# Windowed attention and a GELU MLP on one core: the first MLP product of six of nine tiles by seven block products, and queries and keys handled by pairs of heads

## The chip, the core and the metric

The kernel runs on one core of a Trainium2 chip. The metric is the device time of one execution in microseconds, as the median of several runs; lower is better. A core has five engines with one instruction queue each, worked off in order: TensorE (PE: matmuls, and their weight loads, PEld), VectorE (DVE), ScalarE (ACT), GpSimd (POOL) and SyncE (SP, which only issues DMAs here). They wait for one another through semaphores. Matmul results land in PSUM, which has eight banks of 128 x 512 float32; everything else lies in SBUF or in DRAM.

## What is computed

Eight batches of attention, 8 heads, 576 positions, 64 values per head. Each position sees itself and the 127 before it, with a linear bias per head. The 4608 rows of 512 values that come out go through an MLP of width 2048 with an exact GELU. The core of the reference:

```python
scores = scale * np.matmul(q, k.transpose(0, 1, 3, 2))
mask = (rel >= 0) & (rel < window)                       # window = 128
scores = np.where(mask, scores + bias[None], -1000000000.0)
attn = softmax(scores)
x = np.matmul(attn, v).transpose(0, 2, 1, 3).reshape(B * S, H * D)     # 4608 x 512
h = x @ w_in                                             # 512 x 2048
g = 0.5 * h * (1.0 + erf(h * inv_sqrt2))
return (g @ w_out).astype(np.float32)                    # 2048 x 512
```

## The kernel before

**Two float16 numbers for one float32.** TensorE multiplies float16 at full rate. So nearly every operand is split: it is scaled by a power of two, `hi` is it rounded to float16, `lo` is what is left, rounded to float16 (`low_part`, L144, a DVE operation; `hi` is made by ACT or POOL). A product a*b is then three float16 products, hi*hi + lo*hi + hi*lo, added up in one PSUM bank. The scale comes from the largest absolute value of a whole operand: `absmax` (L212) over each partition, `over_partitions` (L106 to L126) over the 128 partitions, `pow2` (L128) and `inverse` (L138). `over_partitions` of most operands is a chain of small DVE operations: four copies, a reduction, a 32 x 32 transpose, a reduction, a copy, a transpose, and four maxima. Batch 0 of the attention and the second product of tile 0 work in float32.

**The tiles.** The 4608 rows are nine tiles of 512 tokens (`TT`). Tile t needs the attention of batches t - 1 and t, since 576 is more than 512. For each tile there are two stages on TensorE:

- the h stage, `mlp_in` (L577): 16 blocks `fc` of 128 of the 2048 columns. A block takes 12 matmuls (L584) of 128 x 512: four chunks `cc` of the 512 inputs, three products each, into one of the four PSUM banks with the tag `mm`. ACT takes the GELU out of the bank (L600) into a buffer of the tag `ob` (three of them), POOL makes its `hi` (L601), DVE its `lo` (L602, which runs at L145).
- the o stage, `mlp_out` (L612): four blocks `tb` of 128 tokens with 48 matmuls (L622) each, whose results ACT or DVE scale (L630, L632) and SP sends out (L633).

Both stages have 192 matmuls of 128 x 512.

**The attention beside them.** While tile t runs, the attention of batch b = t + 1 is computed. It has four units, one for each pair of heads. A unit is: `scores` (L370), 54 matmuls on quarters of the array (L399) into banks with the tag `att`, five DVE operations that scale them, add the bias and put them into a tile `s` of SBUF (L421); `softmax` (L484), two DVE reductions for the maxima (L491), nine exponentials on ACT (L494), the divisions, `hi` on POOL (L500) and `lo` on DVE (L502), and two transposing DMAs (L503) into `et`; and `weigh` (L515), 54 or more matmuls (L540) whose results go to the tiles `x` of t = b and b + 1 as `hi` by ACT (L553) and `lo` by DVE (L554). The tag `s` has two buffers. ACT has to load another table of functions (ACT_TABLE_LOAD) when it goes from GELU to exponentials or back.

Queries and keys of a batch are loaded whole (L339 to L343: two DMAs into the two buffers of the tag `ld`), and `split_qk` (L345) takes their maxima and splits them into `qbuf` and `kbuf`, 128 x 2304 each, which the units of the batch read.

**What sets the order.** The main loop (L731 to L768) emits the work step by step: step 0 to 15 are `mlp_in`, 16 to 31 quarters of `mlp_out`. `SCORES_AT` and `WEIGH_AT` say at which steps the scores and the weighing of the units are emitted. A scheduler then places the instructions of all engines; by `high_priority` some are moved ahead. What it leaves is a fixed queue for each engine.

## Time and profile before

| | |
|---|---|
| median of 3 runs | 957.98 us (956.48 to 960.62) |
| the profiled execution: its time | 957.65 us |
| its span, first to last instruction | 955.8 us |
| granted TensorE clock, mean | 0.988 |
| DMA moved | 91.18 MB, in 172451 packets |

All times below are of this one execution, counted from the start of its span. The tiles stand in it one behind the other; a tile's h stage begins with its first matmul of L584:

| tile | h stage from | o stage from | until |
|---|---|---|---|
| 0, and all before it | 66.46 | 111.50 | 187.92 |
| 1 | 187.92 | 236.86 | 294.16 |
| 2 | 294.16 | 345.53 | 395.85 |
| 3 | 395.85 | 443.66 | 493.71 |
| 4 | 493.71 | 542.11 | 592.29 |
| 5 | 592.29 | 639.18 | 689.23 |
| 6 | 689.23 | 736.02 | 786.13 |
| 7 | 786.13 | 827.57 | 869.01 |
| 8 | 869.01 | 910.45 | 955.80 |

Tiles 7 and 8 have no attention beside them. How to read the views: the table of windows gives, for each stretch, the busy time of each engine with its number of instructions; a row of the groups gives an instruction's line, engine, operation, operands with shapes, how often, then its busy time and mean duration in ns, and then the idle time of its engine just before it, with what ended it. A matmul's duration includes the time until its result has landed, so matmuls overlap one another, and their pace is the distance of their starts.

### The profile page before, as it was taken

Reading aid. Unit: us, or ns where it says so; the run is one execution under the profiler, and the core shown is the slowest. Engines: PE = TensorE matmul, PEld = TensorE weight load, DVE = VectorE, ACT = ScalarE, POOL = GpSimd, SP = SyncE. Lnnn points to the kernel's source line nnn. Section 1 sums busy time; section 2 is a strip of 40 time slices with the busy share of each in tenths; the row PEclk is TensorE's granted clock in tenths of the full one; section 3 lists DMA queues with packets and bytes.
Section 4 is the critical chain, followed back from the end, with each engine's and each line's share of the span. In section 5 each row is a group of like instructions: output and inputs, shape, how many; then the busy total and the mean of one; then the engine's idle time right before and its main releaser. Section 6 shows DMA issues by size and latency. Waiting matters only on the chain.

```text
span 955.8 us, 17566 instructions
## 1 busy us (share of the span) xinstructions
PE 920.2 (96%) x7036; PEld 450.0 (47%) x7036; DVE 634.8 (66%) x1254; ACT 449.5 (47%) x957; POOL 253.5 (27%) x516
## 2 busy tenths in 40 slices
...
GB/s 324 199 96 244 222 50 74 132 188 100 72 135 166 76 51 106 193 32 66 79 193 45 66 95 171 56 79 95 73 28 51 86 81 1 1 23 23 0 12 34
DMA packets 172451, 91.18 MB, mean 95 GB/s; under 512 B 132561, under 2 KB 153169, under 8 KB 172241
## 3 DMA queue, kind: packets, MB, share of 16 engines
...
## 4 chain that ended last, share of the span: by engine, by line
PE 68%; DVE 8%; ACT 4%; DMA 3%; issue 2%; POOL 1%; SPq 0%; POOLq 0%; ACTq 0%; DVEq 0%
PE o L622 31%; PE h L584 29%; PE av L540 4%; PE sc L399 3%; DMA et<-e_main 2%; ACT s L494 2%; DVE e_main L145 2%; DVE s L421 1%; DVE g L145 1%; DVE nmax L491 1%; DVE stq L213 1%; POOL e_main L500 1%; DMA q<-qp 1%; DVE wo L145 1%; DMA v<-vp 1%
## 5 line engine op out<-in xcount | busy, mean ns | idle before, releaser
L584 PE MATMUL h<-x,wi 128*128 128x512 f16 x1728 | 381.8, 379 | 5.0 <-ACT g L600 3.3
L584 PEld LDWEIGHTS <-wi 128*128 128x128 f16 x1728 | 166.2, 98 | 205.8 <-issue 7.3
L622 PE MATMUL o<-wo,g 128*128 128x512 f16 x1152 | 260.2, 380 | 0.0
L622 PEld LDWEIGHTS <-g 128*128 128x128 f16 x1536 | 145.9, 98 | 175.2 <-issue 0.7
L601 POOL TENSOR_SCALAR g<-g,sg 128x512 f16<-128x512 f32 x128 | 104.2, 818 | 286.1 <-ACT g L600 280.4
L494 ACT ACTIVATE s<-s,nmax 128x192 f32<-128x192 f32 x252 | 111.2, 442 | 121.4 <-DVE nmax L491 114.4
L145 DVE SCALAR_TENSOR_TENSOR g<-g,sg,g 128x512 f16<-128x512 f32 x128 | 106.1, 841 | 90.4 <-POOL g L601 90.3
L500 POOL TENSOR_SCALAR e_main<-s,z 128x192 f16<-128x192 f32 x252 | 121.4, 499 | 126.1 <-issue 43.6
L600 ACT ACTIVATE g<-h,gs 128x512 f32<-128x512 f32 x128 | 86.0, 686 | 135.0 <-PE h L584 108.6
L145 DVE SCALAR_TENSOR_TENSOR e_main<-s,z,e_main 128x192 f16<-128x192 f32 x252 | 111.0, 482 | 15.3 <-POOL e_main L500 14.8
L622 PE MATMUL o<-wo_first,g 128*128 128x512 f16 x384 | 88.3, 379 | 0.0
L399 PE MATMUL sc<-kbuf,qbuf 64*64 64x192 f16 (+1 forms) x1656 | 73.3, 261 | 8.5 <-DMA kbuf<-kp 4.6
L421 DVE SCALAR_TENSOR_TENSOR s<-sc,cs,bias_h 128x384 f32<-128x384 f32 x112 | 63.6, 607 | 12.2 <-PE sc L399 12.0
L553 ACT ACTIVATE x<-av,cx 128x448 f16<-128x448 f32 (+6 forms) x52 | 23.8, 475 | 91.7 <-PE av L540 91.5
L491 DVE TENSOR_REDUCE nmax<-s 128x5 f32<-128x960 f32 (+1 forms) x56 | 58.5, 1044 | 2.7 <-DVE s L421 0.5
L619 PE MATMUL o<-zo,g 128*128 128x512 f32 x128 | 58.1, 606 | 0.0
L540 PE MATMUL av<-et,vbuf 128*64 128x128 f16 (+1 forms) x1680 | 46.0, 215 | 11.9 <-DMA et<-e_main 11.1
L426 POOL MEMSET s<- 64x128 f32 (+1 forms) x112 | 19.1, 171 | 135.1 <-DVE s L421 134.5
L630 ACT ACTIVATE ob<-o,so 128x512 f32<-128x512 f32 x16 | 10.8, 677 | 90.8 <-PE o L622 90.7
L399 PEld LDWEIGHTS <-qbuf 64*64 64x64 f16 x1512 | 36.2, 107 | 36.8 <-issue 33.5
L540 PEld LDWEIGHTS <-vbuf 128*64 128x64 f16 x1680 | 43.0, 114 | 22.2 <-issue 18.4
L632 DVE TENSOR_SCALAR ob<-o,so 128x512 f32<-128x512 f32 x16 | 11.9, 744 | 60.0 <-PE o L622 60.0
...
## 6 DMA issues: line engine op xcount, KB each, us to landing
...
out<-ob SPq DMA_DIRECT2D x36, 256.0 KB, 2.0
...
q<-qp SPq DMA_DIRECT2D x7, 1152.0 KB, 6.1
k<-kp SPq DMA_DIRECT2D x7, 1152.0 KB, 6.0
...
```

Of the source, the lines that this page charges most:

```text
L145: nc.vector.scalar_tensor_tensor(out=dst, in0=src, scalar=scale, in1=high, op0=ALU.mult, op1=ALU.subtract)
L399: nc.tensor.matmul(ps[bank][o, n, 0:W], a, m, start=(i == 0), stop=(i == len(terms) - 1 and b > 0), skip_group_check=True,)
L421: nc.vector.scalar_tensor_tensor(out=s[:, bank[0] : bank[0] + k, :], in0=ps[bank][:, 0:k, 0:W], scalar=cs, in1=bias.broadcast_to([P, k, W] ...
L491: nc.vector.tensor_reduce(out=nmax[:, r], in_=s[:, r], axis=AX.X, op=ALU.max, negate=True)
L494: nc.scalar.activation(s[:, i, :], s[:, i, :], AF.Exp, bias=nmax[:, i : i + 1], accum_out=z[:, i : i + 1])
L500: nc.gpsimd.tensor_scalar(e[:, i, 0, c], s[:, i], z[:, i : i + 1], 1.0, op0=ALU.mult, op1=ALU.mult)
L540: nc.tensor.matmul(av[r, (j - blocks[0]) * QB : (j - blocks[0] + len(js)) * QB], v32s[b][:, hp, kb, r] if b < EXACT else vbuf[:, vi, hp, k ...
L584: nc.tensor.matmul(ph, wi[n][:, a, cc, k * P : (k + 1) * P], x[:, cc, b, :], start=(i == 0), stop=(i == 3 * NCC - 1),)
L600: nc.scalar.activation(g32, ph, AF.Gelu, scale=gsc[t, n])
L601: nc.gpsimd.tensor_scalar(g[:, r, 0], g32, gsg[t, n], 1.0, op0=ALU.mult, op1=ALU.mult)
L619: nc.tensor.matmul(o, g[:, r, c], zo[n][:, n % 2, k * DM : (k + 1) * DM], start=(fc == 0), stop=(fc == NFC - 1))
L622: nc.tensor.matmul(o, g[:, r, a, c], wo[n][:, b, k, :], start=(fc == 0 and i == 0), stop=(fc == NFC - 1 and i == 2),)
```

## The change

**Seven products instead of eight.** From tile 3 on (`FAST`), the h stage is computed for a pair of 256 columns `d` at a time. Its operands are cut into 2 x 2 blocks (input chunks 2i and 2i + 1, first and second 256 tokens, first and second 256 columns), and the four result blocks come from seven block products instead of eight, by sums and differences of blocks. A block product (`add`) is 12 matmuls of 128 x 256: two halves `k` of a bank, two chunks `i`, three float16 products. A tile has 4 x 7 block products with 336 matmuls.

- Four combinations of the weights are made once, during tile 2, in eight calls of `sums_of_weights`: six POOL additions, a rounding by ACT, a DVE subtraction, and four DMAs each. One combination overwrites a block of the weights in SBUF, three go to DRAM (`stored`). In each tile each of the three is read back for each `d` by a DMA of 256 KB (`stream`), 12 for a tile.
- Four combinations of the activations are made for each tile, in two calls of `sums_of_x`: five POOL operations, a rounding by ACT, a DVE subtraction.
- A pair `d` keeps two banks, u and v, over its seven products. P1, P6, P7, P4 go into u one upon the other, and ACT copies u into SBUF after P1 (`s1`), P6 (`s2`) and P7 (`s3`). P2 goes into v, P5 and P3 into v again; after P2, P7 and P3 DVE adds v to `s1`, `s3` and `s2`. The GELU then reads these sums, or u itself after P4.

```python
def p1(self):
    self.u = self.bank("u")
    self.add(self.u, lambda a, i: self.lo[:, a, 2 * i], lambda b, i: self.x[:, 2 * i, b, 0:HT], True)
    self.s1 = self.room("s1")
    nc.scalar.copy(self.s1, self.u)

def p2(self):
    self.v = self.bank("v")
    self.add(self.v, lambda a, i: self.lo[:, a, 2 * i + 1], lambda b, i: self.x[:, 2 * i + 1, b, 0:HT], True)
    nc.vector.tensor_tensor(out=self.s1, in0=self.v, in1=self.s1, op=ALU.add)
    self.out(0, 0, self.s1)

def p6(self):
    self.add(self.u, lambda a, i: streams[T2][:, a, i], lambda b, i: sums[:, i, b, S2], False)
    self.s2 = held2[self.d % 2]
    nc.scalar.copy(self.s2, self.u)
...
    for d in range(len(q)):
        order += [q[d].p1, q[d].p2]
        if d:
            order += [(q[d - 1].p4, T4, d - 1)]
        order += [(q[d].p6, T2, d)]
        if d:
            order += [q[d - 1].p3]
        order += [q[d].p5, (q[d].p7, T3, d)]
    order += [(q[-1].p4, T4, len(q) - 1), q[-1].p3]
```

**Queries and keys by pairs of heads.** From batch 3 on (`WHOLE`), they are loaded, measured and split for one unit at a time (`load_pair`, `stat_pair`, `split_pair`: 128 x 576 each), in halves of `qbuf` and `kbuf`. The buffers of the tag `ld` become one tile `ldbuf`, which from tile 3 on holds the combinations and the streams.

**Maxima over partitions through DRAM.** `over_partitions` (where it was the chain of small DVE operations) becomes two DMAs and two DVE operations:

```diff
-        quarters = small([QP, 8, P // QP], "quarters", 1)
...
-        for k in range(P // QP):
-            nc.vector.tensor_scalar_max(stat[k * QP : (k + 1) * QP, 0:n], back[:, 0:n], FLOOR)
+        rows = dram.tile([P, n], F32, tag=f"rows{n}", name=f"rows{n}", bufs=2)
+        nc.sync.dma_start(rows, stat)
+        flat = every[:, 0 : P * n]
+        nc.sync.dma_start(flat, rows.rearrange("q n -> (q n)")[None, :].broadcast_to([P, P * n]))
+        nc.vector.tensor_reduce(out=stat, in_=flat.rearrange("p (q n) -> p n q", n=n), axis=AX.X, op=ALU.max)
+        nc.vector.tensor_scalar_max(stat, stat, floor)
```

**The order of the attention.** From tile 3 on a tile has 13 steps in its h stage, and the last two products stand in its first two quarters of the o stage. The first unit of batch b is moved into the o stage of the tile before (batch 4 and later), so tile 2 has five units, tiles 3 to 5 four, tile 6 three. The exponentials of the units whose scores stand in an h stage come behind it (`waiting`), with a gate on POOL. Both maxima of a unit stand before its exponentials (`maxima`). The parts that `weigh` writes and the output scaling get `high_priority`. The weights of 512 columns share one scale.

```diff
-    SCORES_AT, WEIGH_AT = (2, 11, 16, 21), (12, 20, 25, 30)
+    AT = ((8, 14, 18, 22), (17, 22, 26, 30)), ((2, 11, 16, 21), (12, 20, 25, 30)), ((4, 8, 15), (14, 19, 22, 25))
+    NEXT_AT = 25
+    SUMS_AT = (4, 6, 8, 10, 12, 14, 16, 18)
```

**Where instructions moved.** Rows of the built programs; in the names the numbers behind a tile are tile and pair `d` (or block), batch and unit, and last a running number. First ACT at the start of tile 4's h stage; before it was:

```order
L630 ACTIVATE ob3_3_5748<-o3_3_5639,so3_4522 128x512
L600 ACT_TABLE_LOAD
L600 ACTIVATE g32_4_0_5771<-h4_0_5757,gs4_0_5751 128x512
L600 ACTIVATE g32_4_1_5788<-h4_1_5775,gs4_0_5751 128x512
L600 ACTIVATE g32_4_2_5816<-h4_2_5803,gs4_0_5751 128x512
L600 ACTIVATE g32_4_3_5864<-h4_3_5851,gs4_0_5751 128x512
L600 ACTIVATE g32_4_4_5890<-h4_4_5876,gs4_0_5751 128x512
L494 ACT_TABLE_LOAD
L494 ACTIVATE s5_0_5820,z5_0_5925<-s5_0_5820,nmax5_0_5924 128x192 x5
L600 ACT_TABLE_LOAD
```

The same place of the changed kernel (L740 rounds the combinations of x, L784, L795 and L803 are the copies of u after P1, P6 and P7, L774 the GELU):

```order
L740 CAST ldbuf_75<-r4_1_6153 128x1024
L784 COPY s14_0_6242<-u4_0_6229 128x512
L774 ACT_TABLE_LOAD
L774 ACTIVATE s14_0_6242<-s14_0_6242,gs4_0_6219 128x512
L795 COPY ldbuf_75<-u4_0_6229 128x512
L803 COPY s34_0_6306<-u4_0_6229 128x512
L784 COPY s14_1_6326<-u4_1_6313 128x512
L774 ACTIVATE s34_0_6306<-s34_0_6306,gs4_0_6219 128x512
L774 ACTIVATE s44_0_6357<-u4_0_6229,gs4_0_6219 128x512
L774 ACTIVATE s14_1_6326<-s14_1_6326,gs4_0_6219 128x512
L795 COPY ldbuf_75<-u4_1_6313 128x512
```

The copies of u stand between the GELUs in one queue, and the exponentials of batch 5 have left the h stage. Next DVE at the same place; before:

```order
L145 SCALAR_TENSOR_TENSOR g4_0_5770<-g32_4_0_5771,sg4_0_5753,g4_0_5770 128x512
L145 SCALAR_TENSOR_TENSOR g4_0_5770<-g32_4_1_5788,sg4_0_5753,g4_0_5770 128x512
L421 SCALAR_TENSOR_TENSOR s5_0_5820<-sc5_0_0_5821,cs5_5534,bias_h_61 128x384
L421 SCALAR_TENSOR_TENSOR s5_0_5820<-sc5_0_2_5822,cs5_5534,bias_h_61 128x384
L213 TENSOR_REDUCE stv6_5996<-v32_6_5794 128x1
L145 SCALAR_TENSOR_TENSOR g4_0_5770<-g32_4_2_5816,sg4_0_5753,g4_0_5770 128x512
L421 SCALAR_TENSOR_TENSOR s5_0_5820<-sc5_0_4_5868,cs5_5534,bias_p_62 128x192
L115 COPY quarters_5998<-stv6_5996 32x1 x3
```

And now (L789 adds v to `s1`, L804 to `s3`; L119 is the reduction that waits for the two DMAs of `over_partitions`):

```order
L741 TENSOR_TENSOR ldbuf_75<-r4_1_6153,ldbuf_75 128x1024
L789 TENSOR_TENSOR s14_0_6242<-v4_0_6244,s14_0_6242 128x512
L217 TENSOR_REDUCE stv6_6527<-v32_6_6289 128x1
L139 SCALAR_TENSOR_TENSOR g4_0_6225<-s14_0_6242,sg4_0_6221,g4_0_6225 128x2x256
L119 TENSOR_REDUCE stv6_6527<-every_70 128x1
L120 TENSOR_SCALAR stv6_6527<-stv6_6527 128x1
L127 TENSOR_SCALAR pwv6_6534<-stv6_6527 128x1
L134 TENSOR_SCALAR scv6_6536<-pwv6_6534 128x1
L330 TENSOR_TENSOR pwx6_6538<-pwv5_5087,pwv6_6534 128x1
L804 TENSOR_TENSOR s34_0_6306<-v4_0_6244,s34_0_6306 128x512
```

One operation stands between the maximum L217 and the reduction L119, and the addition L804, for which TensorE's third product into the bank v waits, stands behind L119. Last SP from the end of tile 3 into tile 4's h stage; before:

```order
L633 DMA out_0<-ob3_2_5636 128x512
L633 DMA out_0<-ob3_3_5748 128x512
L303 DMA v32_6_5794<-vp 128x5x128 x4
L503 DMA_TRANSPOSE et5_0_5926<-e_main_83 128x20x128
L503 DMA_TRANSPOSE et5_0_5926<-e_main_83 128x16x128
```

And now (L116 and L118 are the two DMAs of `over_partitions`, L726 the streams, L373 and L374 a pair's queries and keys):

```order
L116 DMA rows2_6208<-stu24_6206 128x2
L118 DMA every_70<-rows2_6208 128x256
L318 DMA v32_6_6289<-vp 128x5x128 x4
L558 DMA_TRANSPOSE et5_0_6046<-e_main_84 128x16x128
L689 DMA out_0<-ob3_3_6203 128x512
L726 DMA ldbuf_75<-stored_90 128x1024
L116 DMA rows1_6529<-stv6_6527 128x1
L118 DMA every_70<-rows1_6529 128x128
L726 DMA ldbuf_75<-stored_90 128x1024 x5
L374 DMA kbuf_81<-kp 128x576
L726 DMA ldbuf_75<-stored_90 128x1024
L373 DMA kbuf_81<-qp 128x576
```

Streams, loads and the two DMAs of a maximum share one queue, in which L118 waits until L116 has landed.

328 lines of the change are left out of this document (262 added, 66 removed).

## The prediction

> **What bounds the kernel now.** I read the page's busy times and its chain first, then a table of windows with one row for each tile, then the groups.
>
> ```profile
> span 955.8 us, 17566 instructions
> PE 920.2 (96%) x7036; PEld 450.0 (47%) x7036; DVE 634.8 (66%) x1254; ACT 449.5 (47%) x957; POOL 253.5 (27%) x516
> ...
> PE 68%; DVE 8%; ACT 4%; DMA 3%; issue 2%; POOL 1%; SPq 0%; POOLq 0%; ACTq 0%; DVEq 0%
> ```
>
> TensorE is busy for 96% of the span, and 68% of the chain that ended last is TensorE's. The rest of that chain lies mostly ahead of tile 1, which the change hardly touches. So time is won by fewer columns through TensorE, and lost where TensorE has to wait. The table of windows for tiles 1 to 8 (busy time with the number of instructions, then granted clock and DMA):
>
> ```profile
> 187.92:294.16 106.24, 99.16 (x829) 49.23 (x828) 86.46 (x174) 47.59 (x107) 37.07 (x69) 0.98 0.52 132
> 294.16:395.85 101.69, 99.09 (x919) 48.40 (x918) 77.02 (x153) 52.39 (x113) 34.06 (x68) 1.00 0.48 106
> 395.85:493.71 97.86, 97.53 (x818) 47.12 (x817) 74.84 (x150) 50.93 (x112) 32.75 (x68) 1.00 0.43 98
> 493.71:592.29 98.58, 97.15 (x866) 46.94 (x864) 73.94 (x150) 51.52 (x112) 32.56 (x68) 1.00 0.42 97
> 592.29:689.23 96.94, 96.94 (x818) 46.84 (x816) 70.20 (x150) 53.05 (x113) 33.05 (x68) 1.00 0.38 75
> 689.23:786.13 96.90, 96.90 (x841) 46.89 (x840) 57.83 (x111) 45.47 (x109) 32.48 (x68) 1.00 0.30 61
> 786.13:869.01 82.88, 82.88 (x385) 37.56 (x384) 13.74 (x19) 13.65 (x19) 11.15 (x16) 1.00 0.04 13
> 869.01:955.80 86.79, 83.04 (x385) 37.49 (x383) 13.52 (x18) 13.05 (x19) 11.06 (x16) 1.00 0.04 16
> ```
>
> The first number behind the window is its length, the second PE's busy time, the fourth DVE's. Length less PE is PE's idle time: 7.1 us in tile 1, 2.6 in tile 2, 0.3 and 1.4 in tiles 3 and 4, none in tiles 5 to 7. DVE's share of the length is 81% in tile 1, 76, 76, 75, 72 and 60% in tiles 2 to 6. PE's idle time grows with it. That is the scale on which I weigh the added DVE work.
>
> **What the seven products remove.** The pace of matmuls, from the timeline of PE in tile 8, and from a place ahead of tile 1 with matmuls of 384 columns (start, length, operation):
>
> ```profile
> 869.01 41.60 PE L584 MATMUL h<-x,wi 128*128 128x512 f16 x192
> 910.45 2.75 PE L622 MATMUL o<-wo_first,g 128*128 128x512 f16 x12
> ...
> 48.93 1.15 PE L474 MATMUL tp<-bias_h,adders 128*128 128x384 bf16 x6
> ...
> 63.94 0.81 PE L474 MATMUL tp<-bias_h,adders 128*128 128x384 bf16 x4
> ```
>
> 192 matmuls of 512 columns take 910.45 - 869.01 = 41.44 us, 215.8 ns each. Six of 384 columns last 0.34 us longer than four, 170 ns each. No row shows 256 columns. Half of 215.8 is 108 ns, two thirds of 170 is 113; I take 110, nearer to the first, since 0.34 is a difference of rounded numbers. The new stage has 336 of them: 336 x 0.110 = 37.0 us (36.3 to 38.1), which saves 4.5 us a tile (5.2 to 3.4) and 26.9 us in six tiles (31 to 20). At 41.44 / 336 = 123 ns nothing would be saved.
>
> Each new matmul still loads its own weights, so loads rise from 192 to 336 a tile. The group of the attention's weighing shows that short matmuls with a load each do run close together:
>
> ```profile
> L540 PEld LDWEIGHTS <-vbuf 128*64 128x64 f16 x1680 | 43.0, 114 | 22.2 <-issue 18.4
> L540 PE MATMUL av<-et,vbuf 128*64 128x128 f16 (+1 forms) x1680 | 46.0, 215 | 11.9 <-DMA et<-e_main 11.1
> ```
>
> 1680 of them, two side by side, take 46.0 us, 27 ns each, while one load lasts 114 ns: loads overlap. They fill half the array each, so this is not quite the new case. The Trainium skill, in "TensorE: Matmul & The Clock Gate", section "Back-to-back issue gap", has both answers: an isolated gap of N / 2.4 + 2.5 ns, by which an estimate for 256 columns is 109 ns, and a stream of loads and matmuls that at 128 columns is held to about 81 ns instead of 56, because both operations count. By the first the stage would be 36.7 us; the second speaks against this change and is a rival below. The 27 ns a matmul speak for the first.
>
> **What it adds on ACT and DVE.** The groups by form; the two table loads are of tile 4 alone:
>
> ```profile
> L600 ACT ACTIVATE g<-h,gs 128x512 f32<-128x512 f32 x128 | 86.0, 686 | 135.0 <-PE h L584 108.6 <-DVE g L145 17.1 <-DVE sx L140 4.3
> L203 ACT ACTIVATE wi<-zi,sww 128x1024 f16<-128x1024 f32 x8 | 8.9, 1192 | 1.6 <-DVE sww L140 1.6
> L600 ACT ACT_TABLE_LOAD x5 | 6.4, 1283 | 1.0 <-issue 0.9
> L494 ACT ACT_TABLE_LOAD x5 | 6.4, 1283 | 3.6 <-DVE square L116 3.6
> L632 DVE TENSOR_SCALAR ob<-o,so 128x512 f32<-128x512 f32 x16 | 11.9, 744 | 60.0 <-PE o L622 60.0
> L145 DVE SCALAR_TENSOR_TENSOR wo<-zo,s,wo 128x1024 f16<-128x1024 f32 x8 | 10.2, 1294 | 1.3 <-ACT wo L203 1.3
> L453 DVE TENSOR_REDUCE nmax<-sc 128x2 f32<-128x384 f32 x16 | 8.5, 554 | 2.9 <-PE sc L411 2.9
> L126 DVE TENSOR_SCALAR stq<-back 32x2 f32<-32x2 f32 x24 | 5.2, 217 | 0.3
> L115 DVE COPY quarters<-stq 32x2 f32<-32x2 f32 x24 | 4.6, 192 | 0.2
> L122 DVE COPY spread<-top 32x32 f32<-32x32 f32 x12 | 3.1, 258 | 0.1
> L421 DVE SCALAR_TENSOR_TENSOR s<-sc,cs,bias_h 128x384 f32<-128x384 f32 x112 | 63.6, 607 | 12.2 <-PE sc L399 12.0
> L421 DVE SCALAR_TENSOR_TENSOR s<-sc,cs,bias_p 128x192 f32<-128x192 f32 x28 | 11.5, 409 | 10.6 <-PE sc L399 10.5
> L498 DVE RECIPROCAL z<-z 128x5 f32<-128x5 f32 x28 | 5.1, 182 | 0.7
> L213 DVE TENSOR_REDUCE stq<-q 128x1 f32<-128x2304 f32 x7 | 17.8, 2548 | 7.0 <-DMA q<-qp 7.0
> L491 DVE TENSOR_REDUCE nmax<-s 128x5 f32<-128x960 f32 x28 | 32.2, 1150 | 2.4 <-DVE s L421 0.5
> L145 DVE SCALAR_TENSOR_TENSOR e_main<-s,z,e_main 128x192 f16<-128x192 f32 x252 | 111.0, 482 | 15.3 <-POOL e_main L500 14.8
> L399 PE MATMUL sc<-kbuf,qbuf 64*64 64x192 f16 x1512 | 53.9, 249 | 1.3 <-DVE s L421 1.3
> ```
>
> ACT, a tile: 12 copies of u at 0.686 (8.2 us) and two roundings of 1024 values at 1.192, while the gathered exponentials leave 2 of tile 4's 10 table loads, 8 x 1.283 = 10.3 us less. ACT comes out even (8.2 + 2.4 - 10.3), at 51 us of some 95. In the h stage a copy of u has one or two products of 12 x 0.110 = 1.3 us as cover (P2 after P1, P3 and P5 after P6), so I cost the copies at nothing. If ACT comes more than that late, TensorE waits for the difference.
>
> DVE, tiles 3 to 5: 12 additions of a bank at 0.744 are 8.9 us; two subtractions of 1024 values at 1.294 are 2.6; five reductions of a maximum with their floors, at most 0.554 and some 0.15 each (an estimate below the 0.182 of a reciprocal), 3.5; nine more small operations on scales, by the same estimate, 1.4. Two chains of the old `over_partitions` go: four copies at 0.192, four maxima at 0.217 and five single steps of at most 0.258, 2.9 us at most, say 2.2, so 4.4 less. Sum: 12.0. DVE then has 86.8 us in tile 3, 85.9 in tile 4, 82 in tile 5, against PE work of 97 - 4.5 = 92.5: 93, 93 and 89%.
>
> Tile 2 gets a fifth unit, which tile 6 loses. A unit costs DVE 4 x 0.607 + 0.409 for the scores, 1.150 and four fifths of it for the maxima, 9 x 0.44 (111.0 / 252) for the low parts and 4 x 0.18 for the divisions, 9.6 us, and PE 53.9 / 28 = 1.9. With seven of the weights' eight subtractions (9.1), one of x (1.3), a fifth pair to measure and split (half of 2.548, and two of 576 values at some 0.7 by the 0.744 for 512: 2.7) and the statistics (4.2 + 1.4 - 4.4), DVE comes to 77.0 + 23.9 = 101 us, just PE's 99.1 + 1.9.
>
> **POOL and the queues.** A call for the weights or x treats 2048 values.
>
> ```profile
> L601 POOL TENSOR_SCALAR g<-g,sg 128x512 f16<-128x512 f32 x128 | 104.2, 818 | 286.1 <-ACT g L600 280.4 <-DVE turned L118 3.3 <-DVE s L421 2.1
> ...
> out<-ob SPq DMA_DIRECT2D x36, 256.0 KB, 2.0
> q<-qp SPq DMA_DIRECT2D x7, 1152.0 KB, 6.1
> ...
> L503 SPq DMA_TRANSPOSE et<-e_main x56: 1703/2998/5933, 150.6 to 769.9; - x56
> ```
>
> At 0.818 for 512 values a call takes 3.3 us. Tile 2's eight are 26 us on top of 34 on POOL, inside 101. For x the chain from the last weighing is 3.3 + 1.2 (ACT) + 1.3 (DVE) = 5.8 us; its cover is 36 matmuls of the o stage (7.8 us) and P1 and P2 (2.6). So I cost POOL at nothing there. The Trainium skill, in "GPSIMD Engine Reference", section "3.1 Elementwise", measures an addition of two tensors at 4497 ns for 2048 values, against one-input rows like the one above; by that the chain is 7 us, still inside 10.4. No run here shows such an addition yet.
>
> The streams, 256 KB each, land in 2.0 us by the row of `ob`; a buffer is free seven products (9 us) before its next use. That cover is gone if SP's queue stands: it now also holds the two DMAs of each maximum, of which the second waits until the first has landed, and the transposing DMAs, which keep the queue for 3.0 us in the median. Queued behind a late one are streams, hence P6, P7 and P4, and on DVE the additions behind its reduction. I cost it within the idle time that follows.
>
> **The sum.** Where tile 1's idle time went:
>
> ```profile
> PE av L540 <- DMA et<-e_main: 4.1, 1, 4.1
> ```
>
> 4.1 of 7.1 us was one late transposing DMA at the start of the regular attention; 3.0 remain at a DVE share of 81%. For tiles 3 to 5, at about 90%, I take 3.5 us each; for tile 2, with DVE as long as PE, 6; for tile 6 1, for tiles 7 and 8 nothing, and tile 1 and what is ahead of it as before. That is 17.5 us where there were 4.4 in tiles 2 to 6: 13.1 more. 955.8 - 26.9 + 13.1 = 942.0 us of span. The execution's own time is 957.65, 1.85 above its span and 0.3 below the median of 957.98, so I predict 944 us.
>
> **Rivals.**
>
> *The saving in full* (0.20). The idle time stays at 4.4 us: 955.8 - 26.9 + 1.85 = 931 us, and 927 at 108 ns. For it: tiles 5 and 6 had no idle time at DVE shares up to 72%, DVE's work is largely not what PE waits for at once, and the exponentials have left the h stage. Against it: no tile of before ran at 90%.
>
> *The saving eaten by waits* (0.13). Tiles 3 to 5 lose 7.1 us as tile 1 did, tile 2 loses 10, tile 6 1: 32.3, 27.9 more than before, and 955.8 - 26.9 + 27.9 + 1.85 = 959 us, no change.
>
> *The maximum through DRAM holds DVE's queue* (0.16; slower). DVE is in order, and 20 reductions in tiles 2 to 5 wait for two landings, 4.0 us by twice the 2.0 of the row of `ob`, more behind a transposing DMA. In tile 4 only one operation stands between the maximum and its reduction. DVE then sets the length of these tiles: 101 + 87 + 86 + 82 = 356 us and 20 waits w, against 395.1 before, with 15.3 saved in tiles 6 to 8. From w = 2.7 us on the kernel is slower; at 3.5 it has 955.8 + 356 + 70 - 395.1 - 15.3 + 1.85 = 973 us. Against it: most reductions have several operations between.
>
> *Loads are not hidden* (0.03; slower). If each of the 336 loads left 25 ns uncovered, a matmul took 135 ns and the stage 45.4 us, 3.9 more than before: 955.8 + 23.6 + 13.1 + 1.85 = 994 us. This is the skill's second rule; the 27 ns above speak against it.
>
> **How the numbers follow.** The forecast itself has 0.48; its terms alone give 935 to 953. A measurement of this kernel can tell 0.5% from no change: 953.2 and 962.8 us. Faster by more: 0.48 + 0.20 = 0.68; within: 0.13; slower: 0.16 + 0.03 = 0.19. The range 929 to 970 leaves out the lowest part of the first rival and half of the third with the fourth, about 0.2.
>
> **What would show it.** Tiles 7 and 8 must each be 4.5 us shorter, with 256-column matmuls 110 ns apart and no idle time; otherwise the pace is wrong. Tile 2 must be longer than 101.7 us with DVE above 90%; tiles 3 to 5 some 96 us with 3 to 4 us of idle time, before P6 or P5 of a pair or behind the weighing. If DVE idles for the reduction of `every` by 2.7 us and more on average, the third rival holds; if tiles 3 to 5 are shorter than 94 us, the first.

## The result and the profile after

The changed kernel takes 1120.18 us (median of 4 runs, 1117.95 to 1123.05) against 958.91 us before (956.48 to 960.62, 4 runs): a ratio of 1.1686, with an interval of 1.1647 to 1.1724. The forecast of 944 us and its range up to 970 are far off; the kernel is 161 us slower. The profiled execution took 1120.44 us, its span is 1118.7 us.

First the page of the changed kernel: busy times, and the chain that ended last.

```profile
span 1118.7 us, 20035 instructions
...
PE 948.5 (85%) x7900; PEld 554.6 (50%) x7900; DVE 731.5 (65%) x1329; ACT 473.8 (42%) x1049; POOL 371.7 (33%) x633
...
PE 22%; DMA 15%; DVE 14%; ACT 4%; issue 2%; POOL 1%; SPq 1%; DVEq 0%; POOLq 0%; ACTq 0%
```

TensorE was busy for 96% of the span and is now for 85%; its share of the chain fell from 68% to 22%, and DMA and DVE together hold 29%. TensorE's work alone no longer sets the time: the chain goes through its waits for other engines and for DMAs. The table of windows for tiles 1 to 8, as in the prediction (length, PE, PEld, DVE, ACT, POOL, clock, DMA share, GB/s):

```profile
206.71:328.43 121.72, 103.65 (x821) 50.43 (x817) 84.64 (x156) 52.00 (x113) 43.84 (x81) 0.93 0.44 105
328.43:460.00 131.57, 107.40 (x919) 52.24 (x918) 100.16 (x161) 65.79 (x147) 76.44 (x113) 0.92 0.48 111
460.00:593.70 133.70, 105.84 (x962) 65.51 (x961) 90.18 (x178) 47.90 (x123) 47.29 (x85) 0.90 0.52 104
593.70:724.31 130.61, 102.20 (x1009) 64.75 (x1008) 87.31 (x167) 50.26 (x124) 44.69 (x80) 0.90 0.45 103
724.31:854.54 130.23, 103.22 (x961) 64.89 (x960) 87.58 (x168) 50.40 (x124) 45.84 (x81) 0.90 0.44 98
854.54:956.84 102.30, 94.56 (x931) 62.08 (x930) 64.59 (x115) 42.19 (x100) 49.21 (x80) 0.95 0.38 89
956.84:1035.80 78.96, 78.29 (x530) 51.67 (x529) 26.68 (x34) 23.17 (x34) 19.04 (x23) 1.00 0.18 54
1035.80:1118.70 82.90, 78.44 (x529) 51.57 (x527) 22.61 (x30) 19.85 (x31) 11.39 (x16) 0.99 0.15 45
```

Tiles 7 and 8, which have no attention beside them, are 3.9 us shorter each, so the seven products do save. Tiles 3 to 5 should have lasted 96 us and last 130 to 134. DVE's busy time there is 87 to 90 us, close to what the prediction summed up (86.8, 85.9, 82), so the length is not DVE's work. What DVE does in the rest of the tile, the reduction of `every` (line 119 of the changed kernel) shows; its instructions, the idle time ahead of them, and who ended it:

```profile
L119 DVE TENSOR_REDUCE stu<-every x20: 419/420/422, 253.8 to 843.5; 128x2 f32<-128x256 f32 x20
L119 DVE TENSOR_REDUCE stv<-every x6: 285/286/288, 133.2 to 755.1; 128x1 f32<-128x128 f32 x6
...
  DMA every<-rows: 140.0, 27
```

27 reductions of 0.3 to 0.4 us have 140.0 us of idle time ahead of them, 5.2 us each. The issue list gives the landings (KB of one, median us from issue to landing):

```profile
every<-rows SPq DMA_DIRECT2D x21, 128.0 KB, 4.2
...
every<-rows SPq DMA_DIRECT2D x6, 64.0 KB, 5.0
rows<-stu SPq DMA_DIRECT2D x20, 1.0 KB, 3.4
```

One maximum waits for 3.4 us and then 4.2 us. These two are the DMAs alone. From the end of a maximum to its reduction, the 20 of tiles 2 to 5 took 10.0 us in the mean: 1.1 until the first DMA was issued, 4.5 from there until the second was issued, and 4.5 until the reduction began. One such place in tile 4, first on SP's queue (start, length), then DVE, then PE:

```profile
612.93 0.32 SPq L116 DMA_DIRECT2D rows<-stv  x1
620.44 0.32 SPq L118 DMA_DIRECT2D every<-rows  x1
```

```profile
612.82 0.74 DVE L139 SCALAR_TENSOR_TENSOR g<-s,sg,g 128x512 f16<-128x512 f32 x1
625.35 0.29 DVE L119 TENSOR_REDUCE stv<-every 128x1 f32<-128x128 f32 x1 [11.78 <-DMA every<-rows]
...
626.18 0.69 DVE L804 TENSOR_TENSOR s<-v,s 128x512 f32<-128x512 f32 x1
```

```profile
626.92 1.44 PE L763 MATMUL v<-ldbuf,wi 128*128 128x256 f16 x6 [10.20 <-DVE sx L134]
```

The first DMA goes out at 612.93, the second 7.5 us later, since SP's queue stands until the first has landed; that lands 4.9 us later still. DVE idles for 11.78 us with the addition of a bank (line 804) queued behind, and TensorE, which wants that bank for its next product, stands for 10.20 us. The profile names `sx` there, the last of the small steps that the addition was queued among.

The pace of the new products, from PE's timeline at the start of tile 8:

```profile
1035.80 1.47 PE L763 MATMUL u<-x,wi 128*128 128x256 f16 x12
1037.11 1.47 PE L763 MATMUL v<-x,wi 128*128 128x256 f16 x12
```

Twelve start 1.31 us after twelve: 109 ns a matmul, where 110 was forecast.

Not every matmul ran at that pace. The clock in the table of windows is the granted TensorE clock: before, it was 0.98 in tile 1 and 1.00 in tiles 2 to 8, now it is 0.90 to 0.92 in tiles 2 to 5. Two windows of equal length with the new matmuls (L763) alone, the first right behind the wait of 10.20 us above, the second at the start of tile 8 (length, PE, PEld, clock, DMA share, GB/s):

```profile
626.92:629.60 2.68, 2.68 (x13) 1.87 (x13) 0.50 0.00 0
1035.80:1038.48 2.68, 2.68 (x25) 2.41 (x25) 1.00 0.26 98
```

At a granted clock of 0.50, 13 matmuls fill the time of 25. By the clock records of the two traces TensorE was busy at half clock for 109 us in the changed kernel and for 21 us before; half of the difference, some 44 us, is an estimate of what that cost. Each of the 13 stretches at half clock in tiles 3 to 5 begins 2 to 5 us after TensorE has begun to wait, for 1.9 us or more; three other waits there, of 2.2 to 2.8 us, have none behind them. That the waits bring them about is read from this order in time; no run tests it. So a wait of TensorE cost more here than its own length.

### The profile page after: what moved, and what is told of

It is laid out like the page before. It is cut to its first block, busy times and chain, and to the rows that moved or that the text cites. A ratio compares the mean times of both kernels' runs of the same rounds, so it can differ in the third digit from the quotient of the medians.

```text
span 1118.7 us, 20035 instructions
## 1 busy us (share of the span) xinstructions
PE 948.5 (85%) x7900; PEld 554.6 (50%) x7900; DVE 731.5 (65%) x1329; ACT 473.8 (42%) x1049; POOL 371.7 (33%) x633
## 4 chain that ended last, share of the span: by engine, by line
PE 22%; DMA 15%; DVE 14%; ACT 4%; issue 2%; POOL 1%; SPq 1%; DVEq 0%; POOLq 0%; ACTq 0%
PE o L677 10%; PE u L763 6%; DMA every<-rows 5%; PE v L763 5%; DVE e_main L139 4%; DMA rows<-stu 4%; DMA rows<-stv 2%; ACT s L549 2%; DMA v<-vp 2%; DVE s L470 2%; DMA qbuf<-qp 1%; DVE stu L217 1%; DVE nmax L536 1%; DVE g L139 1%; DMA kbuf<-qp 1%
## 5 line engine op out<-in xcount | busy, mean ns | idle before, releaser
L677 PE MATMUL o<-wo,g 128*128 128x512 f16 x1152 | 272.8, 391 | 10.1 <-POOL g L777 8.0
L763 PEld LDWEIGHTS <-wi 128*128 128x128 f16 x1152 | 117.9, 103 | 68.3 <-issue 47.1
L139 DVE SCALAR_TENSOR_TENSOR e_main<-s,z,e_main 128x192 f16<-128x192 f32 x252 | 132.6, 571 | 18.6 <-POOL e_main L555 18.6
L639 PE MATMUL h<-x,wi 128*128 128x512 f16 x576 | 133.1, 389 | 9.6 <-ACT g L652 5.0
L448 PE MATMUL sc<-kbuf,qbuf 64*64 64x192 f16 (+1 forms) x1656 | 83.7, 271 | 42.8 <-DVE s L470 22.4
L763 PEld LDWEIGHTS <-ldbuf 128*128 128x128 f16 x864 | 84.7, 100 | 42.8 <-issue 22.7
L777 POOL TENSOR_SCALAR g<-s,sg 128x512 f16<-128x512 f32 x72 | 54.0, 756 | 137.6 <-ACT s L774 122.9
L763 PE MATMUL v<-ldbuf,wi 128*128 128x256 f16 x576 | 77.8, 293 | 24.5 <-DVE sx L134 18.2
L763 PE MATMUL u<-ldbuf 128*128 128x256 f16 x576 | 76.7, 285 | 22.9 <-ACT s L784 14.8
L139 DVE SCALAR_TENSOR_TENSOR g<-s,sg,g 128x512 f16<-128x512 f32 x72 | 58.8, 832 | 22.0 <-POOL g L777 22.0
L119 DVE TENSOR_REDUCE stu<-every 128x2 f32<-128x256 f32 x20 | 8.4, 420 | 86.4 <-DMA every<-rows 86.4
L774 ACT ACTIVATE s<-s,gs 128x512 f32<-128x512 f32 x48 | 34.4, 720 | 70.0 <-DVE s L804 45.7
```

The costliest lines, as they stand in the source:

```text
L139: nc.vector.scalar_tensor_tensor(out=dst, in0=src, scalar=scale, in1=high, op0=ALU.mult, op1=ALU.subtract)
L448: nc.tensor.matmul(ps[bank][o, n, 0:W], a, m, start=(i == 0), stop=(i == len(terms) - 1 and b > 0), skip_group_check=True,)
L639: nc.tensor.matmul(ph, wi[n][:, a, cc, k * P : (k + 1) * P], x[:, cc, b, :], start=(i == 0), stop=(i == 3 * NCC - 1),)
L677: nc.tensor.matmul(o, g[:, r, a, c], wo[n][:, b, k, :], start=(fc == 0 and i == 0), stop=(fc == NFC - 1 and i == 2),)
L763: nc.tensor.matmul(ps[:, k * HT : (k + 1) * HT], w(a, i)[:, k * P : (k + 1) * P], m(b, i),  start=first and n == 0, stop=True, skip_group_ ...
L774: nc.scalar.activation(room, src, AF.Gelu, scale=gsc[t, 2 * d])
```

## The experiments

All times are medians of 4 runs, with the kernel before beside them on the same chip (956.5 to 958.2 us). Tile lengths are read off the traces, each from its first matmul of the first product to the next tile's:

| kernel | to tile 1 | tile 1 | 2 | 3 | 4 | 5 | 6 | 7 | 8 | span |
|---|---|---|---|---|---|---|---|---|---|---|
| before | 187.9 | 106.2 | 101.7 | 97.9 | 98.6 | 96.9 | 96.9 | 82.9 | 86.8 | 955.8 |
| shared scale, one load buffer, maxima first, priorities (e6) | 196.7 | 104.3 | 103.6 | 98.5 | 98.6 | 97.9 | 96.9 | 82.9 | 86.8 | 966.3 |
| with pairs (e5) | 202.0 | 104.2 | 103.3 | 101.8 | 104.6 | 103.2 | 96.9 | 82.9 | 86.9 | 985.7 |
| with seven products and the units' new places (e1) | 199.6 | 112.2 | 127.6 | 114.9 | 105.0 | 108.1 | 98.2 | 79.0 | 83.0 | 1027.5 |
| changed kernel | 206.7 | 121.7 | 131.6 | 133.7 | 130.6 | 130.2 | 102.3 | 79.0 | 82.9 | 1118.7 |

Each row adds one part of the change to the row above, the last one the maximum through DRAM. So in this order of steps the parts cost 10.5, 19.4, 41.8 and 91.2 us of span. Another order could share the sum out differently. Two things belong to the rows. The places of the units (a fifth unit in tile 2, three in tile 6, exponentials behind the h stage) hang on the tiles with seven products in the text, so e5 and e6 have the old places; the expectation of e5, which says that the new order stays, holds for the maxima and priorities alone. And the mean granted clock of the five profiled executions is 0.988, 0.987, 0.988, 0.960 and 0.929, so the last two steps hold a slower TensorE beside its waits: its busy time is 927.5 us in e1 and 948.5 in the changed kernel.

### The way through DRAM

Theory W is that DVE's wait for the two landings is what costs; its rival H that the rest of the change holds the tiles.

**The old chain put back** (e1). The maximum is taken by the chain of small DVE operations again, in every place; all else is the changed kernel.

```diff
-        rows = dram.tile([P, n], F32, tag=f"rows{n}", name=f"rows{n}", bufs=2)
-        nc.sync.dma_start(rows, stat)
...
-        nc.sync.dma_start(flat, rows.rearrange("q n -> (q n)")[None, :].broadcast_to([P, P * n]))
-        nc.vector.tensor_reduce(out=stat, in_=flat.rearrange("p (q n) -> p n q", n=n), axis=AX.X, op=ALU.max)
...
+        for k in range(P // QP):
+            nc.vector.tensor_copy(quarters[:, 0:n, k], stat[k * QP : (k + 1) * QP, 0:n])
...
+            nc.vector.tensor_scalar_max(stat[k * QP : (k + 1) * QP, 0:n], back[:, 0:n], FLOOR)
```

> The changed kernel with the old chain of small DVE operations as the maximum over partitions; all else as changed. Theory W (DVE waits in its queue for the two DMAs: 140 us of idle time in 27 reductions of the changed kernel's trace): nearly all of the 161 us goes, 935 to 970 us. Rival H (the seven products' banks, handed from TensorE to ACT and DVE and back, make TensorE wait, and the reductions only show it): it stays above 1060 us.

Measured: 1029.64 us, ratio 1.0746 [1.0723, 1.0768]. Neither: the way through DRAM holds 90 us, more than half, but 71 us remain that W did not have.

**The way through DRAM in the kernel before** (e3), which has 12 of these maxima and nothing else of the change.

```diff
-        quarters = small([QP, 8, P // QP], "quarters", 1)
...
+        nc.sync.dma_start(rows, stat)
...
+        nc.sync.dma_start(flat, rows.rearrange("q n -> (q n)")[None, :].broadcast_to([P, P * n]))
```

> The kernel before with the maximum over partitions through DRAM as the only change, 12 of them. W: each holds DVE for some 5 us, of which the tiles' 25 us of DVE slack cover a part: 20 to 60 us slower, 980 to 1020 us. H: within 10 us of before, 950 to 970 us.

Measured: 999.82 us, ratio 1.044 [1.0416, 1.0463]. As W said: 41.7 us for 12, 3.5 us each, net of the chain that goes.

**All maxima by POOL** (e2 in the changed kernel, e4 in the kernel before): `partition_all_reduce`, which the start of the program uses already.

```diff
-        if early:
+        if True:
             nc.gpsimd.partition_all_reduce(stat, stat, P, bass_isa.ReduceOp.max)
```

> The changed kernel with every maximum over partitions taken by one GpSimd operation, as the early ones are, and one DVE operation behind it. W: as with the chain, and a little better, since DVE loses some 40 us of small operations: 925 to 960 us. H: above 1060 us.

> The kernel before with every maximum over partitions by the GpSimd operation. Both theories: 2 to 10 us faster, since DVE loses 12 chains of 2.2 us and PE's idle time in tiles 1 to 4 was 11 us: 948 to 957 us.

Measured: 1261.21 us, ratio 1.3165 [1.3131, 1.3198], and 1010.98 us, ratio 1.0543 [1.0525, 1.0561]. Both expectations were wrong: they counted what DVE loses and gave POOL's side no price. The instruction itself takes 0.37 us. POOL's timeline of e2 around one of them:

```profile
473.12 0.84 POOL L734 TENSOR_TENSOR r<-r 128x256 f32<-128x256 f32 x1
479.94 0.37 POOL L112 PARTITION_ALL_REDUCE stu<-stu  x1 [5.99 <-issue]
...
487.90 0.71 POOL L735 TENSOR_TENSOR r<-r 128x256 f32<-128x256 f32 x1 [7.49 <-issue]
```

POOL stands for 6.0 us ahead of it and for 7.5 us ahead of the next elementwise addition, with nothing in the profile to wait for: 13 us around 0.37. In the kernel before all of them lie at the start, the last at 120.4 us, where POOL has little else to do. The Trainium skill, in "GPSIMD Engine Reference", section "2.1 Instruction dispatch", gives about 6 us for the first call of a freshly loaded routine; here the first figure agrees, and it is paid at nearly every one of these calls between elementwise work, with as much again on the way back; that it is a loading of code is not shown by the trace.

**The two DMAs with nobody waiting.** What do they cost in SP's queue alone? A first try (e8) kept the chain of e1 and issued the DMAs beside it:

```diff
...
+        nc.sync.dma_start(rows, stat)
+        nc.sync.dma_start(every[:, 0:P], rows[:, 0:1].rearrange("q n -> (q n)")[None, :].broadcast_to([P, P]))
         quarters = back_.rearrange("p (n k) -> p n k", n=8)
```

> The kernel with the old chain (1029.6 us), which also issues the two DMAs of every maximum on SP's queue, the first from the maximum to DRAM and the second from there into the buffer of all partitions (64 KB), while nothing waits for what the second brings. Theory A (DVE's wait for the landing is the cost of the way through DRAM): within 10 us of the chain, 1022 to 1040 us. Theory B (SP's queue stands for the first DMA's landing, and what is queued behind it, transposing DMAs, streams and loads, comes late): 1080 us and more, most of the way to the 1120 of the changed kernel.

Measured: 1766.38 us, ratio 1.8438 [1.839, 1.8486]. The experiment failed by its own make: with two columns it picked every other number, so that one broadcast fell into 128 x 128 pieces of 4 bytes. Single issues of SP behind it took 38 us:

```profile
769.07 37.72 SPq L704 DMA_DIRECT2D out<-ob  x1
...
839.69 38.41 SPq L741 DMA_DIRECT2D ldbuf<-stored  x1
```

The second try (e9) takes one piece of 512 bytes a partition, and the chain writes its result into a tile of its own, so that it does not wait for the first DMA's reading. Against e1:

```diff
...
+        half = rows[0 : P // n].rearrange("q n -> (q n)")
+        nc.sync.dma_start(every[:, 0:P], half[None, :].broadcast_to([P, P]))
+        whole = small([P, n], "whole", 2)
...
-            nc.vector.tensor_scalar_max(stat[k * QP : (k + 1) * QP, 0:n], back[:, 0:n], FLOOR)
+            nc.vector.tensor_scalar_max(whole[k * QP : (k + 1) * QP, 0:n], back[:, 0:n], FLOOR)
```

> The kernel with the old chain (1029.6 us), which also issues two DMAs for every maximum on SP's queue while no engine waits for what they bring: the first from the maximum to DRAM, the second, in one piece of 512 bytes for each partition (half of the rows where there are two columns), into the first half of the buffer of all partitions; the chain writes its result into a tile of its own, so that it does not wait for the first DMA to have read. Theory A (DVE's wait for the landings is the cost of the way through DRAM): 1022 to 1045 us. Theory B (SP's queue stands for the first landing, and transposing DMAs, streams and loads behind it come late): 1080 us and more. In the run with pieces of 4 bytes that question was drowned by single SP issues of 38 us.

Measured: 1063.95 us, ratio 1.1123 [1.1083, 1.1163], between the two. The waits of SP and then of PE (tiles 2 to 5) in e9:

```profile
SPq L122 <- DMA rows<-stv: 43.2, 6, 7.6
...
SPq L122 <- DMA rows<-stu: 41.4, 17, 4.2
```

```profile
PE u L781 <- DMA ldbuf<-stored: 13.2, 3, 5.1
PE av L613 <- DMA et<-e_main: 12.0, 3, 10.3
```

SP stands for 85 us for first landings, and TensorE waits in tiles 2 to 5 for 13.2 us for streams, none in e1, and for 12.0 us for transposing DMAs, 7.3 in e1. So of the 90 us some 34 come without any engine waiting for the maximum, and the other 56 with DVE waiting for it. The split is approximate, since e9 keeps the chain's work on DVE and its second DMA brings 64 KB in place of the 128 KB of most maxima. That DVE's wait does hold TensorE is shown at 626.92 above.

### What the rest is made of

**The seven products left out** (e5, on e1), then **the pairs too** (e6): `FAST = 10`, then also `WHOLE = 10` with the loads by whole batches put back.

```diff
-FAST = 3
+FAST = 10
```

> The kernel with the old chain (1029.6 us) without the seven products in any tile: eight products everywhere, no sums of weights or of x, while the pairs and the new order stay. Of the 71 us that the kernel with the old chain is slower than before, its start up to tile 1 holds 11.6, tile 1 6.0, tiles 2 to 5 49.6, tile 6 1.3, and tiles 7 and 8 give 7.8 back. Theory A (the seven products' side work on DVE, ACT and POOL fills DVE to about 90% and makes ACT wait for POOL in its own queue): tiles 3 to 5 come back to 98 to 101 us and tile 2 to 102 to 106, the kernel to 974 to 990 us. Theory B (the pairs, that is smaller units of loading, measuring and halving close ahead of their scores, are what costs): tiles 3 to 5 stay above 104 us and the kernel above 1010 us.

Measured: 988.12 us, ratio 1.031 [1.0278, 1.0341]. Theory A in its main part: the seven products with the units' new places cost 42 us net, 24.3 of them in tile 2 and 18.4 in tiles 3 to 5, where they were to save 13.5. But the pairs are not free: tiles 3 to 5 keep 101.8 to 104.6 us, above the range of theory A.

> As the pairs-only kernel, but queries and keys loaded and halved by whole batches as before: what is left of the change is the shared scale of two blocks of weights, the one buffer for loads, both maxima of a unit ahead of its exponentials, and the higher priority of the copies behind the weighing and the second product. Theory A (these set the 17.6 us that the start and tile 1 lose): 970 to 982 us, with tiles 2 to 6 within 2 us of before each. Theory B (the start loses because of DMAs or loads of the pairs, or of the seven products): within 5 us of before, 953 to 963 us.

Measured: 970.22 us, ratio 1.0129 [1.0104, 1.0155]: theory A. Nearly all of it lies ahead of tile 1.

**Seven products in the last two tiles alone** (e7), on the kernel before: `FAST = 7`, whole loads, the old order of maxima and exponentials; the shared scale and the one buffer for loads stay.

> The kernel before, with seven products in the last two tiles alone: maxima by the old chain, queries and keys by whole batches, the order of maxima and exponentials as before; the sums of weights and of tile 7's x are made in tile 6, whose DVE was busy for 60%. Tiles 7 and 8 gave 3.9 us each in three runs so far, so if tile 6 hides the sums (49 us of POOL beside 32, some 12 of DVE beside 58): 948 to 953 us. If the start loses as in the other kernels because of the shared scale of the weights and the one buffer for loads: 960 to 972 us.

Measured: 985.94 us, ratio 1.029 [1.0265, 1.0315], worse than both cases. Tile 1 begins 15.4 us late, and tile 6, which makes the sums, takes 109.2 us instead of 96.9. DVE's busy time in tile 6 rose from 57.83 to 78.18 us by this row of e7, 20 us where 12 were counted:

```profile
708.40:817.60 109.20, 100.97 (x841) 48.17 (x840) 78.18 (x119) 52.44 (x117) 75.38 (x111) 0.97 0.40 96
```

**The shared scale alone** (e16), on the kernel before.

```diff
-        pow2_of_words(pww[:, r], stat)
-        inverse(sww[:, r], pww[:, r])
+        nc.vector.tensor_tensor(out=stat[:, 0:1], in0=stat[:, 0:1], in1=stat[:, 1:2], op=ALU.max)
+        pow2_of_words(pww[:, r], stat[:, 0:1].broadcast_to([P, len(ns)]))
+        inverse(sww[:, r], pww[:, r], 12)
```

> The kernel before with the shared scale of two blocks of weights alone (one more small step of DVE for each pair of blocks at the start, and other powers of two in the scales), no other edit: the loads, the maxima, the products and the order of the text are as before. Theory A (that step comes late in DVE's full queue of tile 0 and sets the start): tile 1 starts at 194 us or later, 964 to 974 us in all. Theory B (the one buffer for loads and the earlier maxima and scales change the order of the start): 954 to 962 us.

Measured: 974.43 us, ratio 1.0173 [1.0133, 1.0212]: theory A, at the upper edge of its range. Four small operations move the start of tile 1 from 187.9 to 204.4 us.

**Its chain as short as before** (e11, on e6): floor and maximum in one operation, and the scales of tile 0 block by block again.

```diff
+        nc.vector.scalar_tensor_tensor(
+            out=stat[:, 0:1], in0=stat[:, 0:1], scalar=STAT_FLOOR, in1=stat[:, 1:2], op0=ALU.max, op1=ALU.max
+        )
```

> The kernel with the order alone (970.2 us), whose start up to tile 1 is 8.7 us longer than before. Here the floor and the maximum over the two blocks are one operation instead of two, and the scales of tile 0 are made block by block in the loop again, so that the chain from the maximum to the halves of a pair of weights has as many steps on DVE as before. Theory A (each further small step of that chain takes a place of its own in DVE's full queue, behind operations of 1.2 us): tile 1 starts at 187 to 192 us and the kernel takes 957 to 964 us. Theory B (the one buffer for loads or the earlier maxima do it): 968 us and more.

Measured: 977.27 us, ratio 1.0211 [1.0181, 1.0241]. Theory A falls: tile 1 begins at 198.1 us, and takes 113.3 itself. The edit of the scale alone is enough to delay the start (e16), but not by the number of its steps; whether the one buffer for loads and the earlier maxima have a part in e6 and e11 is not shown. In tile 0 DVE is busy for 112 of 121 us in the kernel before, and by the traces its operations there stand in another order in each of e6, e11 and e16; which move of it costs the time stays open.

### Why the seven products lose

Open were three causes: ACT's waits for POOL, DVE's own added work, and POOL's additions themselves. In e1's tile 2 ACT stands for the sums of the weights:

```profile
ACT ldbuf L731 <- POOL ldbuf L728: 28.0, 4, 13.6
```

**Rounding on POOL** (e12, on e1) takes ACT out of it.

```diff
-        nc.scalar.copy(hi, flat)
+        nc.gpsimd.tensor_copy(hi, flat)
```

> The kernel with the old chain (1029.6 us), with the high halves of all sums, of weights and of x, rounded by a copy on POOL instead of ACT. Theory A (ACT, which takes its queue in order, stands for POOL's additions: 28.0 us in tile 2 and 16.4 us in tile 3 of that kernel, and what is queued behind it comes late): tile 2, 127.6 us there, falls below 120 and tile 3, 114.9 us there, below 110; the kernel takes 1005 to 1020 us. Theory B (POOL's own length and its effect on DVE is what costs): POOL has 1.5 to 2 us more for each of the 20 calls, and the kernel takes 1025 us or more.

Measured: 1031.52 us, ratio 1.0767 [1.0726, 1.0807]: theory B, no change. ACT's waits alone don't hold the 42 us. POOL has the roundings as additional work here, so a part of them that this work eats up again isn't excluded.

**A load on POOL alone.** The first try (e10) put 96 additions that read only weights into the text of tiles 3 to 5 of the kernel before.

> The kernel before, with 96 additions of two tensors on POOL in each of tiles 3, 4 and 5, 128 columns each, read from weights and written to a place that nobody reads, so that no other engine waits for them except through POOL's queue: some 45 us more of POOL a tile, about what eight calls for the sums of the weights took. Theory A (POOL's and DVE's operations on two tensors in SBUF slow each other): the low parts of g, 812 ns where POOL is quiet, go to 950 ns or more in these tiles, and the tiles grow by 2 to 6 us each, 963 to 977 us in all. Theory B (only DVE's own added work and ACT's waits for POOL's results cost time): the low parts stay within 5% and the kernel within 5 us of before.

Measured: 1045.22 us, ratio 1.0916 [1.0883, 1.095], but not of what was asked: nothing tied the additions to their tiles, and the scheduler moved all of them into tile 0, where POOL had to change to the reductions over partitions and back four times, at some 6 and 7 us. Tiles 2 to 8 are as before. The second try (e13) reads the tile's own x.

```diff
+            if 3 <= t <= 5 and step in (4, 6, 8, 10, 12, 14, 16, 18):
+                x, spare = x_tile(t), ident32.bitcast(F16)
+                for n in range(8):
+                    c, a = divmod(n, 2)
+                    nc.gpsimd.tensor_tensor(out=spare, in0=x[:, c, a, 0:256], in1=x[:, c, a, 256:512], op=ALU.add)
```

> The kernel before, with 64 additions of two tensors on POOL for each of tiles 3, 4 and 5, 256 columns of f16 each, read from that tile's x (so that they can't run before its weighings) and written to a place that nobody reads; some 0.7 us each, 45 us more of POOL a tile. In the first try at this all additions, which read weights alone, ran in tile 0. Theory A (POOL's work stretches those DVE operations that read two tensors of SBUF, or copy or scale from SBUF to SBUF, and no others): where the additions run, the low parts of e_main go from 0.45 to 0.55 us or more, the divisions of z from 0.17 to 0.3 or more, while maxima (1.15 us) and the sums with the scores' banks (0.61 us) stay; DVE grows by 6 to 12 us a tile, the kernel by 4 to 15 us to 962 to 973. Theory B (only DVE's own added work and waits for POOL's results cost time): no form changes by more than 10%, and the kernel stays within 4 us of before.

Measured: 996.97 us, ratio 1.0408 [1.0374, 1.0442], more than either theory had. Tiles 3, 4 and 5 take 110.8, 111.8 and 110.9 us, 13 to 14 more each, all other tiles are within 0.5 of before from tile 1 on. DVE's groups in tile 4, first of the kernel before (count, busy, mean ns):

```profile
L145 DVE SCALAR_TENSOR_TENSOR e_main<-s,z,e_main 128x192 f16<-128x192 f32 x36 | 15.8, 483 | 1.2 <-POOL e_main L500 1.2
...
L421 DVE SCALAR_TENSOR_TENSOR s<-sc,cs,bias_h 128x384 f32<-128x384 f32 x16 | 9.1, 606 | 2.1 <-PE sc L399 2.1
L491 DVE TENSOR_REDUCE nmax<-s 128x5 f32<-128x960 f32 x4 | 4.6, 1154 | 0.3
...
L497 DVE TENSOR_SCALAR z<-z 128x4 f32<-128x4 f32 x4 | 0.7, 181 | 1.8 <-ACT s L494 1.8
...
L115 DVE COPY quarters<-stq 32x2 f32<-32x2 f32 x4 | 0.6, 146 | 0.0
```

And in e13:

```profile
L145 DVE SCALAR_TENSOR_TENSOR e_main<-s,z,e_main 128x192 f16<-128x192 f32 x36 | 18.3, 554 | 2.3 <-POOL e_main L500 2.3
...
L421 DVE SCALAR_TENSOR_TENSOR s<-sc,cs,bias_h 128x384 f32<-128x384 f32 x16 | 9.0, 603 | 0.0
L491 DVE TENSOR_REDUCE nmax<-s 128x5 f32<-128x960 f32 x4 | 4.6, 1151 | 0.6 <-POOL s L426 0.4
...
L115 DVE COPY quarters<-stq 32x2 f32<-32x2 f32 x4 | 2.0, 500 | 0.0
...
L497 DVE TENSOR_SCALAR z<-z 128x4 f32<-128x4 f32 x4 | 1.7, 425 | 1.1 <-ACT s L494 1.1
```

A copy of 64 values takes 500 ns instead of 146, a scaling of `z` 425 instead of 181, the low part of `e_main` 554 instead of 483, and the reductions (1151) and the scores out of a bank (603) what they took. The Trainium skill, in "SBUF — State Buffer", section "Who interferes with whom", says that DVE's copies and scalings in their fast modes, and its operations on two tensors of SBUF, share a port with GpSimd and block, while reductions never do; these rows agree. Sorted by what POOL did meanwhile, in tiles 3 to 5 of e13, a low part of `e_main` took 410 ns where POOL did nothing and 767 beside one of the additions; copies of 32 values took 139 ns even there. DVE's busy time grew by 7 to 9 us a tile. Beside it, DVE's wait for POOL's high half of g rose from 7.3 us in tiles 3 to 5 before to 32.4; TensorE was busy for some 4 us more a tile, at a granted clock of 0.95 to 0.97 where it had 1.00; and ACT's x twice waited for the added readers, 15.3 us, which the change itself would not do. So the 13 us are too much for the change by up to 5, and how they divide among the others was not tried.

**The sums left out** (e14 without those of the weights, e15 also without those of x; both on e1). Their products are of other numbers than the reference's; only their time is of use.

```diff
-        nc.scalar.copy(hi, flat)
-        nc.vector.tensor_tensor(out=lo, in0=flat, in1=hi, op=ALU.subtract)
...
+        for n in (T2, T3, T4):
+            nc.sync.dma_start(stored[n, d, :, :, i], wi[2 * d + 1][:, :, 2 * i])
```

> The kernel with the old chain (1029.6 us) with the sums of the weights left out: no additions on POOL, no roundings on ACT and no subtractions on DVE for them in tile 2; the stored streams are copies of two blocks of weights, and the DMAs stay but for the one back into a block. Its products are therefore of other numbers. Theory A (the sums' POOL work, through DVE, is what makes tile 2 24 us longer than with the pairs alone): tile 2 falls from 127.6 to 103 to 110 us, the rest stays, and the kernel takes 1004 to 1016 us. Theory B (the fifth unit and the order do it): tile 2 stays above 116 us, the kernel above 1017.

Measured: 1003.81 us, ratio 1.0487 [1.0448, 1.0526]: theory A in the total, 26 us back, for POOL's additions, ACT's roundings and DVE's eight subtractions together. Tile 2 falls to 111.2, a little above its range, and tile 1 by 7 to 105.1, since the first calls were placed there.

> As the last, and without the sums of x as well: they are filled once with a copy of x of the fourth tile, and the seven products of all tiles read that. DVE and POOL have 2.6 and 10.8 us less in each of tiles 3 to 5. Theory A (POOL's additions and what they stretch on DVE set the length of these tiles): tiles 3 to 5 (114.9, 105.0 and 108.1 us) fall to 97 to 101 us each, the kernel to 975 to 990 us. Theory B (the 12 copies on ACT and 12 additions on DVE of a bank in each tile, and the order of the units, hold them): they stay above 103 us, the kernel above 992.

Measured: 990.02 us, ratio 1.034 [1.0298, 1.0381]: at the upper edge of theory A's range by the total, by theory B in the tiles. Tiles 3 to 5 take 108.4, 106.3 and 106.0 us. So, against e14, the sums of x hold 3.8 us of tile 2, 5.3 of tile 3 and 5.8 of tile 6, and 2 at most of tiles 4 and 5. There the rest of the seven products still costs more than it saves: 106 us against 104.6 and 103.2 with the pairs alone. It has 12 additions of a bank on DVE, 0.68 us each, and 12 copies on ACT in each tile, and the units' new places; which of them it is wasn't tried. Tile 2 keeps 4.1 us above the pairs alone, with the fifth unit in it.

**The additions on DVE** (e17, on e1): `nc.gpsimd.tensor_tensor` becomes `nc.vector.tensor_tensor` in both functions of sums.

> The kernel with the old chain (1029.6 us), with all additions of the sums, of weights and of x, on DVE instead of POOL. By 0.68 us for an addition of 512 values, and half and a little for 256, a call for weights costs DVE 3.0 us and a call for x 3.0 us: 24 us in tile 2 and 6 in each later tile, while POOL loses 49 and 11. Theory A (an operation of POOL costs DVE and POOL's own queue about as much as it takes): tile 2 (127.6 us) stays within 6 us and tiles 3 to 5 (114.9, 105.0, 108.1) fall or stay, 1015 to 1036 us in all. Theory B (DVE's own length sets these tiles, and POOL's load is nearly free): tile 2 above 138 us, tiles 3 to 5 longer by 4 us or more each, the kernel above 1045.

Measured: 1020.23 us, ratio 1.0638 [1.0584, 1.0691]: theory A in the total. By tiles it was off: tile 2 falls to 115.7, tile 3 rises to 123.5; taken together they are 3 us shorter. The addition of 1024 values, first by POOL in e1, then by DVE in e17:

```profile
L744 POOL TENSOR_TENSOR r<-x 128x1024 f32<-128x1024 f16 x12 | 26.1, 2180 | 13.5 <-DVE x L151 5.6 <-DVE top L126 3.3 <-DVE z L565 2.8
```

```profile
L744 DVE TENSOR_TENSOR r<-x 128x1024 f32<-128x1024 f16 x12 | 15.0, 1256 | 0.1
```

The fuller engine does it in 0.58 of the time, and the kernel is 9 us the better for it.

No version tried beats the kernel before. The whole saving of the two tiles where it comes free is 7.8 us, and the shared scale that it needs came with a start of tile 1 that was 9 to 19 us later in every kernel that had it.

## Why the prediction was wrong, point by point

**The pace and the saving: right.** 109 ns instead of 110; tiles 7 and 8 gained 3.9 us each where 4.5 were forecast. The loads are hidden, and the fourth rival is out.

**DVE's work: right within 6 us.** 100.2, 90.2, 87.3 and 87.6 us in tiles 2 to 5, against 101, 86.8, 85.9 and 82. Of what the sum lacks, the low parts of `e_main` hold some 3 us a tile: they took 571 ns each in the changed kernel and 482 before.

**"I cost it within the idle time that follows": wrong, the first failing step.** This put the two DMAs of each maximum into 6 us of idle time in tile 2 and 3.5 in the others. The landing of 2.0 us was read from the outputs' row, though the same list has 4.7 and 5.0 us for the 288 KB loads of queries and keys; the two landings took 3.4 and 4.2 us in the median, with a queue between them that stands. 20 maxima in tiles 2 to 5 held DVE for 112 us, 5.6 each. These are DVE's waits in the changed kernel from 328.43 to 854.54 (us in all, times, longest):

```profile
DVE stu L119 <- DMA every<-rows: 74.3, 16, 12.0
DVE stv L119 <- DMA every<-rows: 37.9, 4, 11.8
```

The third rival had the mechanism, and its test, 2.7 us, was passed by far; it got 0.16 because "most reductions have several operations between". That is so: 18 of the 20 had 3 to 19 operations between. But these cover 4.6 us in the mean, of a way of 10.0. By its own sum w = 5.6 gives 955.8 + 356 + 112 - 395.1 - 15.3 + 1.85 = 1015 us; what lies between that and 1120 is in the next points and in DVE's waits for other engines, 49 us in tiles 2 to 5. The price of this step, by experiment, is 90 us.

**"So I cost POOL at nothing there": wrong, the second failing step.** It asked whether POOL's chain ends in time, for a call alone in POOL's queue. A call for x took 5.4 us (2.18 and four of 0.8 by the rows of e1) instead of 3.3, which would still be inside its cover. But at the start of tile 4, four roundings of the attention stand in the middle of the second call; POOL, ACT, PE:

```profile
594.45 2.12 POOL L732 TENSOR_TENSOR r<-x 128x1024 f32<-128x1024 f16 x1 [1.41 <-DVE z L553]
596.54 4.38 POOL L555 TENSOR_SCALAR e_main<-s,z 128x192 f16<-128x192 f32 x4
...
603.39 0.72 POOL L737 TENSOR_TENSOR r<-r 128x256 f32<-128x256 f32 x1
```

```profile
604.15 1.04 ACT L740 CAST ldbuf<-r 128x1024 f16<-128x1024 f32 x1 [7.60 <-POOL r L737]
605.10 0.58 ACT L784 COPY s<-u 128x512 f32<-128x512 f32 x1
```

```profile
605.73 1.23 PE L763 MATMUL u<-ldbuf 128*128 128x256 f16 x5 [7.50 <-ACT s L784]
```

ACT stands 7.60 us for the call, the copy of u behind it, and TensorE 7.50 us; at the start of tile 5 it is 7.3 us, of tile 3 3.2. Nor did the step ask what POOL's work does to DVE. A load of 42 to 49 us a tile on POOL lengthens tiles that have nothing else changed by 13 us (e13), and the sums of the weights held 26 us of the kernel (e14).

**"Tile 1 and what is ahead of it as before": wrong, the third.** Tile 1 begins 18.8 us later and takes 15.5 us more. The shared scale alone, on the kernel before, moves that start by 16.5 us (e16), with the other edits of e6 by 8.8; tile 1 has calls for weights (7.1 us) and 9.5 us by the way through DRAM.

**A wait at its own length: mis-sized, the fourth.** The sum adds idle time to TensorE's work at full pace. Of the 177 us between the forecast span of 942.0 and the measured 1118.7, 121 are more idle time of TensorE (170 us, where the forecast had 49), and 55 are a longer busy time (948.5 us, where 920.2 - 26.9 = 893 were forecast), some 44 of it by the half clock, as estimated with the result.

**The pairs: mis-sized.** They stood within DVE's sum; by experiment they cost 19 us, 5 ahead of tile 1 and 3 to 6 in each of tiles 3 to 5 at a DVE share near 80%, where the forecast had counted 3.5 us of idle time for everything together. In that experiment their five maxima a tile went by the chain, not through DRAM.

**ACT's copies: right for the copies themselves, as far as shown.** TensorE waited for them for 14.8 us in the changed kernel, at the two places where ACT stood for POOL ahead of the copy, and for 5.6 us in tiles 3 to 5 of e1.
